# Attention and two expert layers in one kernel: first weight splits of a block placed earlier, and the repeat rounds put under a condition

## The chip, the cores and the metric

The kernel runs on one core of a Trainium2 chip. The metric is device time in microseconds of one execution, the median of three runs; lower is better.

## The reference

Three layers follow each other on 1792 tokens (4 batches of 448) with 768 features; everything is float32, except that the two weights of the first expert layer arrive as float64.

- Attention with 12 heads of 64: `scores = scale * q k^T`, mixed over heads by `w_pre`, softmax, mixed over heads by `w_post`, times `v`.
- First layer ("moe1" in the code): `h = x @ w_in` (768 x 2048), `g = h - tanh(h)`, `x = g @ w_out` (2048 x 768).
- Second layer ("moe2"): every token goes to one of 8 experts (the largest of 8 logits); `out = gate * (relu(x @ w1[e]) @ w2[e])` with 1024 hidden features.

## The kernel before, in words

Most operands are split in a high and a low part (`x = hi + lo`), and one product becomes three matmuls: hi times hi, hi times lo, lo times hi. ScalarE (ACT) writes the high part by a copy, VectorE (DVE) or GpSimd (POOL) subtracts it from the original.

**Attention** ends with a stretch called `window(3)`: 6 pairs of heads, 24 matmuls each (L304). ACT evicts each result twice (L309, L311), POOL subtracts (L312), SyncE (SP) stores both parts to `xd` in DRAM (L357).

**moe1** works in four blocks of tokens (512, 512, 512, 256), and each block in 16 units `f`, one for each 128 hidden features. For unit `f`: `first(b, f)` (L623) is 18 matmuls of `x` with `w_in` (L628) into one of two PSUM banks; `shape(b, f, h)` (L631) computes `h - tanh(h)` by four ACT operations (L638 to L641) and six DVE operations (L642 to L650), and splits the result (ACT L654, POOL L655 in block 0); `second(b, f)` (L665) is 18 matmuls with `w_out` (L672). The loop at L909 runs over the units; in the pass of unit `i` it issues `first` and `shape` of unit `i` and `second` of unit `i - 2`. The bank of `h` is given back when DVE has done L643 of that unit, and `first` two units later writes it again.

Block 0 also brings the weights in. `load_wi(f)` (L475) starts two loads, `wih` and `wil`, the parts of `w_in` that attention stored. `load_wo(f)` (L489) starts the load of `w_out` as float64 into `wor`, of which there is one buffer (only units 1, 14 and 15 have other room), and converts it to float32 by three DVE operations (`convert_f64`, L74: L77, L79, L81); the next `wor` load starts when L81 has read the buffer. `split_wo(0, f)` (L506) then makes `whl`: ACT L509 copies, DVE L510 subtracts.

**What sets the order.** Each engine works its instructions in one fixed order. A scheduler in the language picks it: an instruction takes the place of its line in the program, `tc.high_priority(offset=n)` moves it forward by n instructions, `tc.issue_after(x)` puts it behind `x` where both are on one engine, and otherwise it goes where the scheduler's own estimate has it ready. Before the loop, L570 to L578 issue with priority 300: `x` of block 0, `w_in` of units 0 and 1, `w_out` of units 0 and 1 with their conversions. `split_wo(0, 0)` (L907) and `split_wo(0, 1)` (L920, in the pass of unit 0) come with no priority. `prepare_turn` (L614, in the pass of unit 1) has six small PE transposes (L617) of the expert embedding and one DVE copy of them (L621) with priority 150. `behind(n)` (L500) puts what it holds behind the n-th last unit that was shaped.

**moe2** gathers the tokens of each expert and works through `one_round` (L1003). Each engine's last instructions are those of L1264 and L1267: `count(25, 1)` loads a flag from SBUF into a register of each engine, and a loop that runs zero or one times holds nine inner loops with further rounds, for experts with more tokens than the windows hold. With these inputs the flag is zero, and the loop is passed over. The last work before it is the scatter of output rows by POOL (L1159).

Of the kernel before, what the change touches and what calls it, by code (L numbers as in the profile page):

```python
# [11 lines left out]
F32 = mybir.dt.float32  # L12
# [3 lines left out]
I64 = mybir.dt.int64  # L16
AF = mybir.ActivationFunctionType
ALU = mybir.AluOpType
# [6 lines left out]
DM = H * D  # L25
# [3 lines left out]
FC = DFF // 128  # L29
# [420 lines left out]
def moe1(tc, ctx, bank, xd, wind, sums, w_out, emb, tau, consts, yg, pos, keep, ids0, chosen, w12):  # L450

    nc = tc.nc
    lasting, weights = ExitStack(), ExitStack()

    def pool(name, bufs, side):
        stack = lasting if side == "left" else weights
        return stack.enter_context(tc.tile_pool(name=name, bufs=bufs, side=side, reuse_waits="tile"))
# [3 lines left out]
    pv, pw = pool("m1v", 1, "right"), pool("m1w", 1, "right")  # L461
# [3 lines left out]
    X, G, Y, YT, W = {}, {}, {}, {}, {}  # L465
    wih, wil, wo = {}, {}, {}
# [22 lines left out]
    def load_wo(f):  # L489
        raw = W.get(("raw", f))  # L490
        if raw is None:
            raw = pv.tile([128, DM], I64, tag="wor", name=f"wor_{f}")
            chosen["wor"] = nc.sync.dma_start(out=raw, in_=w_out[f])
        wo[f] = (pw if f < FC - 1 else p1).tile([128, DM], F32, tag=f"wo{f}", name=f"wo_{f}")
        with behind(9 if f > FC - 3 else 99):
            chosen["wo", f] = convert_f64(nc, raw, wo[f])

    steps = []

    def behind(n):  # L500
        order = ExitStack()
        for x in steps[-n] if len(steps) >= n else ():
            order.enter_context(tc.issue_after(x.ins))
        return order

    def split_wo(b, f):  # L506
        if b == 0:
            w = p3.tile([128, 2, DM], F32R, tag="whl", name=f"whl_{b}_{f}")
            nc.scalar.copy(w[:, 0], wo[f])  # L509
            nc.vector.tensor_tensor(out=w[:, 1], in0=wo[f], in1=w[:, 0].bitcast(F32), op=ALU.subtract)  # L510
            W[b, f] = w[:, 0], w[:, 1]
        elif b == 1:
            if f in (0, FC - 4, FC - 2):
                W["pairs"] = p3.tile([128, 2, DM], F32R, tag="whl", name=f"whl_{b}_{f}")
            if 0 < f < FC - 4:
                w = pw.tile([128, DM], F32, tag=f"wo{f - 1}", name=f"wp_{f}")
            else:
                w = W["pairs"][:, f % 2]
            w = w.bitcast(F16)
            W[b, f] = w[:, :DM], w[:, DM:].bitcast(BF)  # L520
            with behind(2):
                nc.scalar.copy(W[b, f][0], wo[f])
                nc.gpsimd.tensor_tensor(out=W[b, f][1], in0=wo[f], in1=W[b, f][0], op=ALU.subtract)
        else:
            W[b, f] = W[1, f]
# [5 lines left out]
    def weigh(f):  # L531
        nc.scalar.activation(out=sq.bitcast(BF), in_=wih[f].rearrange("p a b -> p (a b)"), func=AF.Square,
                             accum_out=room[:, f:f + 1])
# [36 lines left out]
    with tc.high_priority(offset=300):  # L570
        load_x(0)
        load_wi(0)
        load_wi(1)
        load_wo(0)
        raw = px.tile([128, CC, 512], BF, tag="xl", name="wor_1")
        W["raw", 1] = raw.rearrange("p a b -> p (a b)").bitcast(I64)[:, :DM]
        nc.sync.dma_start(out=W["raw", 1], in_=w_out[1])
        load_wo(1)  # L578

    sq = cp.tile([128, DM], F16, tag="sq", name="sq")  # L580
    rt = cp.tile([128, 2], F32, tag="rt", name="rt")
    en = cp.tile([128, CC, 32], F32, tag="en", name="en")
# [31 lines left out]
    def prepare_turn():  # L614
        pt = bank(0, CC - 1, 6)
        for c in range(CC):
            nc.tensor.transpose(pt[:, 8 * c:8 * c + 8], em[:, 128 * c:128 * c + 128], ident[:8, :8])  # L617
        with tc.high_priority(offset=150):
            with tc.issue_after(chosen["wo", 1].ins):
                nc.vector.memset(en, 0.0)  # L620
            nc.vector.tensor_copy(en[:, :, :8], pt[:, :48].rearrange("p (a b) -> p a b", b=8))  # L621

    def first(b, f):  # L623
        N = BLOCKS[b][1]
# [279 lines left out]

    chosen["kept"] = {}
    units = [(b, f) for b in range(len(BLOCKS)) for f in range(FC)]
    split_wo(0, 0)  # L907
    todo = []
    for i, (b, f) in enumerate(units):  # L909
        if b == 0 and 0 < f < FC - 1:  # L910
            load_wo(f + 1)
        with tc.issue_after(chosen["wor"].ins):
            if b == 0 and f + 2 < FC:
                load_wi(f + 2)
            if f == 2 and b + 1 < len(BLOCKS):
                load_x(b + 1)
            if b == 0 and f == 3:
                load_last()
        if i + 1 < len(units):
            split_wo(*units[i + 1])  # L920
        h = first(b, f)
        with tc.issue_after(chosen["wo", 1].ins):
            if b == 0 or f != 1:
                shape(b, f, h)
        if b == 0 and 3 <= f < FC - 1:
            for k in (2 * f - 6, 2 * f - 5) if f < 7 else (f + 1,):
                with behind(2):
                    weigh(k)
        if b + 1 < len(BLOCKS) and 8 <= f < 8 + CC:
            with behind(2):  # L930
                highest(b + 1, f - 8)
        if b + 1 < len(BLOCKS) and f == FC - 2:
            with behind(2):
                bound(b + 1)
        if i == 1:
            prepare_turn()
            for t, src in ((rt[:, 0:1], tau), (lt, tri_d)):
                nc.sync.dma_start(out=t, in_=src)
        if i == 4:
            with behind(2):  # L940
                prepare()
        if todo and (b != 1 or f > 5):
            g, a = todo.pop(0)
            g(*a)
        if i >= 2:
            second(*units[i - 2])
            if units[i - 2][1] == FC - 1:
                with ExitStack() as order:
                    for x in drain(units[i - 2][0]):
                        order.enter_context(tc.issue_after(x.ins))  # L950
                    shape(b, f, h)
                todo = routing(units[i - 2][0])
        for _ in range(1 if b < len(BLOCKS) - 1 else 2):
            if todo and f >= (6 if b == 1 else 2):
                g, a = todo.pop(0)
                g(*a)
        if b == len(BLOCKS) - 1 and f == 5:
            fetch_early()
        if b == len(BLOCKS) - 1 and 6 <= f < 10:
            with behind(2):  # L960
                split_early(2 * (f - 6))
                split_early(2 * (f - 6) + 1)
        if i == len(units) - 3:
            assert not todo
            weights.close()
        if i >= len(units) - 3:
            yield
# [11 lines left out]
def moe2(tc, ctx, bank, ident, yg, pos, keep, ids0, chosen, w12, out, before):  # L979
    nc = tc.nc  # L980
# [22 lines left out]
    def one_round(lists, wins, offs, nm, before=None):  # L1003
# [70 lines left out]
        def split(e, f, j):  # L1074
            if wins[e] == LATE or (before and (e, f, j) in early):
                RW[e, f, j] = kept[f, j]
                return
            raw = RW[e, f, j]
            if before and e == 0:
                wh, wl = lasting(f, j)  # L1080
            else:
                wh = p3.tile([128, DM], F16, tag=f"wh{j}", name=f"wh{j}_{nm}_{e}_{f}")
                wl = p3.tile([128, DM], BF, tag=f"wl{j}", name=f"wl{j}_{nm}_{e}_{f}")
            nc.scalar.copy(wh, raw)  # L1084
            pool_part = (f, j) in ((2, 1), (3, 0), (4, 0), (6, 1)) if before and e == 0 else (f + 2 * j) % 4 == 0
            s = (nc.gpsimd if pool_part else nc.vector).tensor_tensor(out=wl, in0=raw, in1=wh, op=ALU.subtract)  # L1086
            if pool_part:
                chosen["pool"] = s
            RW[e, f, j] = (wh, wl)

        def first(e, f):
# [45 lines left out]
        OR, sent = {}, []  # L1137
# [27 lines left out]
        units = [(e, f) for e in range(E) for f in range(MF)]  # L1165
# [10 lines left out]
        def behind(*ins):  # L1176
            order = ExitStack()
            for x in ins:
                if x is not None:
                    order.enter_context(tc.issue_after(x.ins))  # L1180
            return order
# [17 lines left out]
        for i, (e, f) in enumerate(units):  # L1199
# [1 line left out]
            if f == 0 and e + 1 < E and e + 1 < len(lists):  # L1201
                gather(e + 1)
            if before and e == E - 1 and f == 0:
                with behind(chosen["pool"], sent[-1]):
                    nc.gpsimd.drain(fusable=False)
            if i + 1 < len(units):
                with ExitStack() as order:
# [55 lines left out]
    def count(i, top):  # L1263
        return nc.values_load(keep[0:1, i:i + 1], min_val=0, max_val=top,  # L1264
                              skip_runtime_bounds_check_because="a count of comparisons")

    with tc.For_i(0, count(25, 1)):  # L1267
        for i, (k, n) in enumerate(wins):
            with tc.For_i(0, count(16 + ranks[i], NMORE)) as rd:
                one_round([lists[i]], [MORE], [k * n + rd * MW], f"b{i}")  # L1270
# [94 lines left out]
```

## Time and profile before

| | us |
|---|---|
| median of three runs | 1212.46 (1210.51 to 1213.22) |
| the profiled execution | 1210.71 |
| its span, first to last instruction | 1208.9 |
| TensorE busy in the span | 1162.2 (96%) |
| VectorE busy | 851.1 (70%) |
| ScalarE busy | 748.2 (62%) |
| GpSimd busy | 560.9 (46%) |

The mean granted clock of TensorE over the span is 0.992 of full speed. How to read it: the span is 1.8 us shorter than the time of its own execution, and that execution was 1.75 us faster than the median. Attention takes the first 458 us or so, moe1 lies between 441 and 928 us with its block 0 up to about 602 us, moe2 takes the rest. Busy shares are means over all stages; what a stage waits for is read from the timeline of that stage.

### The profile page before, as it was taken

The numbers are of one execution on the slowest core, as the hardware profiler recorded it, in microseconds if no ns is written. First come the engines' busy times: TensorE is split into PE (matmuls) and PEld (weight loads), VectorE is DVE, ScalarE is ACT, GpSimd is POOL, SyncE is SP. The second block draws the span as 40 slices with busy tenths as digits, with TensorE's granted clock in tenths as the row PEclk, the third lists the DMA queues.
The fourth block names the chain that finished last, engine by engine and source line by source line (L and its number), as shares of the span: only waits on it lengthen the run. The fifth ranks groups of instructions, "written<-read, shape, count | busy, mean of one in ns | idle before, by whom it ended". The sixth has DMA issues, their size and how long they took to land. (4 is left out here: it accounts for less than half of the span.)

```text
span 1208.9 us, 23922 instructions
## 1 busy us (share of the span) xinstructions
PE 1162.2 (96%) x8648; PEld 773.1 (64%) x8648; DVE 851.1 (70%) x2002; ACT 748.2 (62%) x1554; POOL 560.9 (46%) x514
## 2 busy tenths in 40 slices
PE   8999999999999988999999999999999899999996
PEld 3655655665565664665644444544787778899994
DVE  5888779778877875999766766565676655566772
ACT  6887688778868754655565655554577334555661
POOL 3897588678858772111334322111223233344431
PEclk8999999999999999999999999999999999999998
DMA  6465667566665465533100020010034656678760
GB/s 204 148 208 174 195 196 212 163 192 195 195 191 172 151 199 169 206 120 129 55 1 1 1 81 1 1 53 3 2 121 171 215 194 198 212 251 270 248 239 24
DMA packets 84601, 174.13 MB, mean 144 GB/s; under 512 B 12747, under 2 KB 62155, under 8 KB 84472
## 3 DMA queue, kind: packets, MB, share of 16 engines
q1 hardware_dynamic: 78730, 160.95, 40.8%
q0 software_dynamic: 5472, 11.43, 3.5%
q8 instruction: 70, 1.15, 0.4%
q14 instruction: 59, 0.48, 0.2%
q10 hardware_dynamic: 270, 0.12, 0.0%
HBM read 110.98 MB, written 23.30 MB: 111 GB/s over the span
## 5 line engine op out<-in xcount | busy, mean ns | idle before, releaser
L294 POOL TENSOR_TENSOR at<-at 128x480 f16<-128x480 f32 x180 | 179.6, 1008 | 41.3 <-ACT at L293 37.7
L239 PE MATMUL bank<-G,wmix 120*120 120x448 f32 x360 | 171.1, 560 | 8.6 <-DMA G<-S 8.6
L289 PE MATMUL bank<-wr,A 120*128 120x120 f32 (+4 forms) x1800 | 169.9, 242 | 5.4 <-DVE wr L271 4.1
L660 POOL TENSOR_TENSOR ghl<-g,ghl 128x512 bf16<-128x512 f32 (+1 forms) x48 | 48.3, 1006 | 221.5 <-ACT ghl L659 191.1
L249 ACT ACTIVATE A<-bank,st 120x448 f32<-120x448 f32 x180 | 114.9, 638 | 51.7 <-DVE st L243 24.8
L243 DVE TENSOR_REDUCE st<-bank 120x1 f32<-120x448 f32 x180 | 111.6, 620 | 49.5 <-PE bank L239 47.4
L672 PE MATMUL bank<-ghl,whl 128*128 128x512 f32 (+2 forms) x558 | 124.1, 374 | 2.6 <-POOL ghl L655 1.4
L628 PEld LDWEIGHTS <-wih 128*128 128x128 f16 x768 | 73.8, 98 | 74.1 <-issue 10.1
L293 ACT COPY at<-bank 128x480 f32<-128x480 f32 x180 | 101.7, 567 | 29.4 <-PE bank L289 29.1
L1084 ACT CAST wh_a<-wr_a 128x768 f16<-128x768 f32 x112 | 92.6, 829 | 40.2 <-PE bank L1122 33.5
L672 PE MATMUL bank<-ghl,wp 128*128 128x512 f16 (+3 forms) x594 | 113.3, 344 | 1.4 <-POOL ghl L660 1.1
L289 PEld LDWEIGHTS bank<-wr,A 120*128 120x128 f32 (+1 forms) x720 | 90.6, 191 | 37.1 <-issue 19.1
L1086 DVE TENSOR_TENSOR wl_a<-wr_a,wh_a 128x768 bf16<-128x768 f32 x84 | 83.3, 992 | 30.4 <-ACT wh_a L1084 30.1
L254 POOL TENSOR_TENSOR A<-A 120x448 f16<-120x448 f32 (+1 forms) x90 | 85.2, 946 | 28.5 <-ACT A L249 15.0
L642 DVE SCALAR_TENSOR_TENSOR g<-bank,u 128x512 f32<-128x512 f32 (+1 forms) x64 | 39.8, 622 | 81.1 <-ACT d L639 76.9
L658 ACT ACTIVATE g<-g,scales 128x512 f32<-128x512 f32 (+1 forms) x48 | 31.2, 650 | 96.5 <-DVE g L650 83.3
L672 PEld LDWEIGHTS <-wp 128*128 128x128 f16 (+1 forms) x594 | 57.9, 98 | 49.0 <-issue 2.2
L628 PE MATMUL bank<-mxh,wih 128*128 128x512 f16 (+1 forms) x384 | 84.5, 357 | 4.3 <-DVE d L643 4.3
L1122 PE MATMUL bank<-rh_a,wl_a 128*128 128x208 f16 (+5 forms) x336 | 86.2, 260 | 0.0
L1122 PE MATMUL bank<-rl_a,wh_a 128*128 128x208 bf16 (+5 forms) x336 | 86.2, 260 | 0.0
L1098 PE MATMUL bank<-xph_a,wh_a 128*128 128x208 f16 (+5 forms) x336 | 86.2, 259 | 0.0
L1122 PE MATMUL bank<-rh_a,wh_a 128*128 128x208 f16 (+5 forms) x336 | 86.2, 259 | 0.0
(249 smaller groups left out, 2758.8 us busy)
## 6 DMA issues: line engine op xcount, KB each, us to landing
wr_a<-in_w_dram SPq DMA_DIRECT2D x62, 768.0 KB
G<-S SPq DMA_DIRECT2D x176, 210.0 KB
raw_w<-in_w_in_dram SPq DMA_DIRECT2D x32, 384.0 KB
wor<-in_w_out_dram SPq DMA_DIRECT2D x14, 768.0 KB
raw_v<-in_v_dram SPq DMA_DIRECT2D x16, 384.0 KB
yg<-row SPq DMA_DIRECT2D x3, 1540.0 KB
raw_q<-in_q_dram SPq DMA_DIRECT2D x9, 448.0 KB
raw_k<-in_k_dram SPq DMA_DIRECT2D x9, 448.0 KB
```

The source lines that it names most:

```text
L239: nc.tensor.matmul(ps[:r, :S], wmix[:r, :r], g[:r], start=True, stop=True)
L243: latest["dve"] = nc.vector.tensor_reduce(out=st[:r, k:k + 1], in_=ps[:r, :S], axis=AX.X, op=ALU.min)
L249: latest["act"] = nc.scalar.activation(out=a[:r, :S], in_=ps[:r, :S], func=AF.Exp, bias=bias, scale=-1.0, accum_out=st[:r, 4 + k:5 + k])
L254: nc.gpsimd.tensor_tensor(out=parts[1][:r, :S], in0=a[:r, :S], in1=parts[0][:r, :S], op=ALU.subtract)
L289: nc.tensor.matmul(ps[:, jc * r:jc * r + r], x[:r, js], w[:r].rearrange("p (a b) -> p a b", b=10)[:, :, :n], start=(i == 0), stop=(i == le ...
L293: nc.scalar.copy(at32[:, :, t0:t0 + n], v)
L294: nc.gpsimd.tensor_tensor(out=atl[:, :, t0:t0 + n], in0=at32[:, :, t0:t0 + n], in1=ath[:, :, t0:t0 + n], op=ALU.subtract)
L628: nc.tensor.matmul(h, u[f][:, c], X[b][v][:, c, :N], start=(i == 0), stop=(i == len(seq) - 1))
L672: chosen["second"] = nc.tensor.matmul(Y[b][c][:, :N], w[u][:, 128 * c:128 * c + 128], hl[v], start=(f == 0 and i == 0), stop=(f == FC - 1 ...
L1084: nc.scalar.copy(wh, raw)
L1098: nc.tensor.matmul(h, w[u][:, 128 * c:128 * c + 128], XP[e][v][:, c, :N], start=(i == 0), stop=(i == len(seq) - 1))
L1122: nc.tensor.matmul(O[e][c][:, :N], w[u][:, 128 * c:128 * c + 128], r[v], start=(f == 0 and i == 0), stop=(f == MF - 1 and i == 2))
```

## The change

The splits of units 0 and 1 move into the high-priority stretch before the loop, together with the loads of `w_in` and `w_out` for unit 2; the loop no longer issues these. The conversion of `w_out` for unit 2 is put behind the shaping of unit 0. All of `shape` is put behind both splits (on ACT and DVE), and the DVE copy of the transposed embedding behind the last DVE operation of unit 0. The loop around the further rounds becomes a condition, with the rounds as the block that is placed next. The key `"pool"` is renamed `"low"` where it held an instruction, which changes nothing that runs.

```diff
@@ load_wo
-        with behind(9 if f > FC - 3 else 99):
+        with behind(9 if f > FC - 3 else 1 if f == 2 else 99):
             chosen["wo", f] = convert_f64(nc, raw, wo[f])
@@ split_wo
             w = p3.tile([128, 2, DM], F32R, tag="whl", name=f"whl_{b}_{f}")
-            nc.scalar.copy(w[:, 0], wo[f])
-            nc.vector.tensor_tensor(out=w[:, 1], in0=wo[f], in1=w[:, 0].bitcast(F32), op=ALU.subtract)
+            chosen["split", f] = (nc.scalar.copy(w[:, 0], wo[f]), nc.vector.tensor_tensor(
+                out=w[:, 1], in0=wo[f], in1=w[:, 0].bitcast(F32), op=ALU.subtract))
@@ in the stretch with priority 300
         load_wo(1)
+        load_wi(2)
+        W["raw", 2] = pv.tile([128, DM], I64, tag="wor", name="wor_2")
+        chosen["wor"] = nc.sync.dma_start(out=W["raw", 2], in_=w_out[2])
+        split_wo(0, 0)
+        split_wo(0, 1)
@@ prepare_turn
-            nc.vector.tensor_copy(en[:, :, :8], pt[:, :48].rearrange("p (a b) -> p a b", b=8))
+            with tc.issue_after(steps[0][0].ins):
+                nc.vector.tensor_copy(en[:, :, :8], pt[:, :48].rearrange("p (a b) -> p a b", b=8))
@@ the loop over units
-    split_wo(0, 0)
...
-            if b == 0 and f + 2 < FC:
+            if b == 0 and 0 < f < FC - 2:
                 load_wi(f + 2)
...
-        if i + 1 < len(units):
+        if 0 < i < len(units) - 1:
             split_wo(*units[i + 1])
         h = first(b, f)
-        with tc.issue_after(chosen["wo", 1].ins):
-            if b == 0 or f != 1:
+        if b == 0 or f != 1:
+            with ExitStack() as order:
+                for x in chosen["split", 0] + chosen["split", 1]:
+                    order.enter_context(tc.issue_after(x.ins))
                 shape(b, f, h)
@@ moe2, the end
-    with tc.For_i(0, count(25, 1)):
+    more = count(25, 1)
+    with tc.If(more > 0, preferred_fallthrough_block=True):
         for i, (k, n) in enumerate(wins):
```

## Rows read from the trace of the kernel before

**Rows 1.** The page, part 1: busy time, share of the span, instructions
```profile
PE 1162.2 (96%) x8648; PEld 773.1 (64%) x8648; DVE 851.1 (70%) x2002; ACT 748.2 (62%) x1554; POOL 560.9 (46%) x514
```

**Rows 2.** Stretches of 5 us: busy of PE, PEld, DVE, ACT, POOL; clock, DMA, GB/s
```profile
455.00:460.00 5.00, 5.00 (x44) 2.88 (x39) 0.22 (x1) 1.96 (x4) 2.45 (x5) 1.00 0.28 93
...
465.00:470.00 5.00, 1.11 (x9) 0.72 (x9) 3.33 (x6) 2.54 (x4) 0.00 (x0) 0.92 0.22 81
470.00:475.00 5.00, 3.91 (x11) 1.29 (x10) 5.00 (x9) 2.90 (x4) 1.28 (x1) 0.73 0.09 16
```

**Rows 3.** Timeline of PE, block 0: start, length, what, [idle before, releaser]
```profile
464.93 0.54 PE L617 MATMUL bank<-ident,em_stage 8*128 8x8 f32 x6
469.36 2.72 PE L628 MATMUL bank<-mxh,wih 128*128 128x512 f16 x6 [3.89 <-DVE d L643]
...
488.69 1.47 PE L628 MATMUL bank<-mxh,wih 128*128 128x512 f16 x6
...
496.70 1.47 PE L628 MATMUL bank<-mxh,wih 128*128 128x512 f16 x6
```

**Rows 4.** Timeline of DVE, from the first conversions to unit 0's last step
```profile
449.39 3.52 DVE L81 SCALAR_TENSOR_TENSOR wo<-wor,wo 128x768 uint32<-128x768 uint32 x2
458.60 0.22 DVE L620 MEMSET en<- 128x192 f32 x1 [5.70 <-POOL bp L569]
462.27 0.69 DVE L642 SCALAR_TENSOR_TENSOR g<-bank,u 128x512 f32<-128x512 f32 x1 [3.45 <-ACT d L639]
465.50 0.21 DVE L621 COPY en<-bank 128x48 f32<-128x48 f32 x1 [2.54 <-PE bank L617]
466.88 1.83 DVE L510 TENSOR_TENSOR whl<-wo,whl 128x768 fp32r<-128x768 f32 x2 [1.16 <-ACT whl L509]
468.62 0.68 DVE L643 SCALAR_TENSOR_TENSOR d<-bank,d 128x512 f32<-128x512 f32 x1
...
472.10 0.73 DVE L650 COPY_PREDICATED g<-u,d 128x512 f32<-128x512 int32 x1
```

**Rows 5.** Timeline of PE's weight loads, the first of unit 2
```profile
466.53 0.10 PEld L628 LDWEIGHTS <-wih 128*128 128x128 f16 x1 [1.16 <-DMA wih<-wind]
```

**Rows 6.** Timeline of SP: loads of float64 weights for units 3, 9 and 13
```profile
473.69 0.33 SPq L493 DMA_DIRECT2D wor<-in_w_out_dram  x1
...
526.43 0.33 SPq L493 DMA_DIRECT2D wor<-in_w_out_dram  x1
...
559.39 0.33 SPq L493 DMA_DIRECT2D wor<-in_w_out_dram  x1
```

**Rows 7.** Timeline of DVE, the conversion of unit 9
```profile
530.91 0.82 DVE L77 TENSOR_SCALAR wo<-wor 128x768 uint32<-128x768 uint32 x1 [1.09 <-DMA wor<-in_w_out_dram]
```

**Rows 8.** Waits of DVE, 475 to 600 us: total, times, longest
```profile
DVE wo L77 <- DMA wor<-in_w_out_dram: 2.3, 4, 1.1
```

**Rows 9.** Timeline of PE, block 0, `second` of unit 10
```profile
557.61 4.15 PE L672 MATMUL bank<-ghl,whl 128*128 128x512 f32 x17 [0.52 <-POOL ghl L655]
```

**Rows 10.** Timeline of POOL, the last scatter
```profile
1198.50 0.93 POOL L1159 DMA_INDIRECT out_dram<-or_a,oi_a  x1 [5.92 <-ACTq L1267]
```

**Rows 11.** Line 1267 in stretches of 1 us: ns min/median/max, first and last start
```profile
L1267 PEldq COMPARE_BRANCH  x1: 3867/3867/3867, 1197.4 to 1197.4; - x1
...
L1267 POOLq COMPARE_BRANCH  x1: 53/53/53, 1198.9 to 1198.9; - x1
...
L1267 POOLq EVENT_SEMAPHORE  x3: 43/43/43, 1201.7 to 1201.9; - x3
...
L1267 POOLq COMPARE_BRANCH  x1: 41/41/41, 1202.3 to 1202.3; - x1
...
L1267 POOLq EVENT_SEMAPHORE  x9: 43/43/43, 1205.3 to 1206.0; - x9
...
L1267 POOLq COMPARE_BRANCH  x1: 33/33/33, 1207.6 to 1207.6; - x1
```

**Rows 12.** DMA queues, 1202 to 1203 us: packets, MB, share of 16 engines
```profile
q14 instruction: 2, 0.02, 6.7%
```

More of the change, by code (lines that the diff above doesn't have):

```diff
@@ L1087, in split @@
             if pool_part:
-                chosen["pool"] = s
+                chosen["low"] = s
             RW[e, f, j] = (wh, wl)
@@ L1203, in one_round @@
             if before and e == E - 1 and f == 0:
-                with behind(chosen["pool"], sent[-1]):
+                with behind(chosen["low"], sent[-1]):
                     nc.gpsimd.drain(fusable=False)
```

## The prediction

> **What bounds the kernel now.** The page comes first: TensorE is busy 96% of the span [rows 1], so time can only come from the few places where it stands still. The waits of PE by stretch lead to the one large place after attention, the start of moe1, and the table of 5 us stretches shows it: from 465 to 470 us PE is busy 1.11 us, from 470 to 475 us 3.91 us, at a mean granted clock of 0.92 and 0.73 between its levels of 1.2 and 2.4 GHz, where it was 1.00 before the stop [rows 2]. The second place is the end: POOL finishes its scatter at 1199.43 us [rows 10], yet the span goes on to 1208.9.
>
> The timeline of PE tells what the first place costs. The six small transposes end at 465.47; the first matmul of unit 2 starts at 469.36, held 3.89 us by DVE's L643, which gives the PSUM bank of unit 0 back. At 488.69 `first` of unit 4 starts. In between lie two `first` and two `second`, 72 matmuls. One of each, from 488.69 to 496.70, takes 8.01 us, so 16.0 of these 23.2 us are work, and **7.2 us** are lost to the stop, to the lower clock and to late operands [rows 3].
>
> The timeline of DVE tells why. ACT's `d` let L642 run at 462.27, so L643 could have followed at about 462.9. But the embedding's copy stood ahead of it and waited 2.54 us for PE's transposes, then both splits, which waited 1.16 us for ACT's copies and took 1.7; L643 came at 468.62. Meanwhile DVE had stood idle 5.70 us before 458.60 and 3.45 us before 462.27, with both conversions done by 452.91 [rows 4]. The `w_in` of unit 2 was late too: PE's weight load waited for it until 466.53 [rows 5].
>
> A third reading decides how much of the 7.2 us stays. In the middle of block 0 the loads of float64 weights follow each other in a loop, conversion, load, conversion. From unit 9 to 13 four turns take 32.96 us, 8.24 each [rows 6], longer than PE's 8.01. The load takes 4.48 us (526.43 to 530.91), the conversion among `shape`'s steps the rest, and DVE sometimes waits for the load [rows 7, 8]. By unit 10 PE has no lead left: `second` waits 0.52 us for `ghl` [rows 9]. So at the end of this stretch PE can be only as much earlier as this loop is.
>
> **The change, part by part.**
>
> *Splits, copy, order.* The two splits move into DVE's and ACT's idle time. From 455 to 460 us ACT is busy 1.96 of 5 us and DVE 0.22 [rows 2], and they need 1.83 us of DVE [rows 4] and about as much of ACT. POOL's memset at about 458.5, for which DVE's L620 waited, suggests that the room of moe1's left pools comes free only when attention's last matmuls end. Then the splits run from 458.5 to 462, still ahead of L642. If they start earlier, ACT's copies stand between evictions of attention with over half of ACT free; I price that at nothing, at most at 1 us. L643 then comes at 462.9, 5.7 us earlier, and `first` of unit 2 starts behind the transposes at about 465.5. Unit 0's last step, L650, comes 3.5 us after L643, as before (472.10 less 468.62), so it ends at 463 + 3.5 + 0.7 = 467 or sooner. The embedding's copy follows it; its bank is used only by the sixth group of `second`, over 4 us later, so it costs nothing.
>
> *Loads of unit 2.* Two loads of `w_in`, 192 KB each, and one of float64 weights move ahead on SP. The first two end the wait of 1.16 us [rows 5], which lay inside the 3.89 us. The third waits for the conversion of unit 0, at worst until 452.91 [rows 4], with attention's stores behind it on SP; their data is read in later blocks, so I take nothing, and 1 us as the bound.
>
> *Conversion of unit 2.* It waits for L650 of unit 0 and needs 2.4 us of DVE, with up to 1.2 us of unit 1's steps between: it ends at 469 to 470.5. The load of unit 3 followed it at 473.69 [rows 6], and so moves forward by 3.2 to 4.7 us; a shorter unit 0 would add about 1. I take **4.7 us** for this loop and, by the third reading, for block 0. The bounds are 0, if the loop keeps its place, and 7.2, if it closes up. Behind block 0 PE is busy nearly throughout and its inputs shift with it, so the gain stays.
>
> *The condition at the end.* POOL's sequence before: a branch at 1198.9, then waits for the scatter's landing until 1201.9, a branch at 1202.3, nothing until 1205.3, semaphore instructions to 1206.2, nothing until a branch at 1207.6, the end at 1208.9 [rows 11]. The first pause, 3.0 us, is a far jump over the rounds: two packets of instructions were fetched on a queue at that moment [rows 12], and PE's branch of the same kind took 3.87 us, hidden at 1197.4 behind the wait for the scatter [rows 11]. With the rounds placed next, the far jump must be the first branch, at 1198.9, ahead of the wait; 3.0 us later it is 1201.9, just when the scatter has landed. I take 3.0 for that pause and 1.0 of the 1.4 and 0.9 us behind it, **4.0 us**. The bounds are 0 and 5.3: after 1202.3 nothing is left then but the 1.3 us from 1207.6 to the end.
>
> The trace gives the branches themselves 33 to 53 ns on POOL [rows 11] and the pause behind the second 3.0 us. The Trainium skill, Advanced Engine Details and Errata, section Control Flow Timing, has a compare-and-branch at about 108 ns; by that figure alone moving the branch gives 0.1 us at the end, and the sum would be 4.8 instead of 8.7, an estimate from that page.
>
> **Sum:** 4.7 + 4.0 = 8.7 us. Against the profiled execution, 1210.71, that is 1202.0; it ran 1.75 us under the median shown. On the median of 1212.46 it is **1203.8 us**.
>
> **The rivals.** A measurement of this kernel tells 0.2% from no change, 2.4 us: faster is under 1210.0, slower over 1214.9.
>
> *The loop keeps its place.* PE gains 7 us at unit 2 and gives them back as waits for `ghl` in units 5 to 12, because the conversions stay where they were. For it: the 8.24 against 8.01 us and the wait of 0.52. Against it: the loop's start hangs on unit 0's steps, which move. Block 0 then gives 0.8, the sum is 4.8, the time 1207.7.
>
> *The jump is not hidden.* POOL makes a far jump behind the scatter's landing after all, or one more on the way to the end. Against it: POOL's first branch stands ahead of the landing. The time is 1212.46 - 4.7 = 1207.8. The rule of the Trainium skill, Runtime: NRT & Kernel Launch, section Instruction fetch mechanics, speaks for it: a taken branch to code that is not held stalls until it is fetched, and with the rounds next it is the path always taken here that jumps. The 3.0 and 3.87 us agree with the rule; whether the wait hides them no row shows.
>
> *Nothing moves.* The scheduler keeps the splits behind unit 0's steps or trades one stop for another, and the end keeps its pauses: 1211.5.
>
> *Slower: DVE stands before its loads.* DVE's order in block 0 is written anew. If each conversion now stands before more of `shape` and reaches its load sooner, DVE idles there, and it has no time to spare. Before, it waited 2.3 us in all [rows 8]. There are 11 conversions from unit 3 on; an added wait of 0.8 us each uses up the 8.7 us, and at 1.2 us each the time is 1212.46 + 13.2 - 8.7 = 1217. Against it: the same rules order these steps as before, and the load and what stands behind it shift together.
>
> **How the numbers follow.** Forecast 0.58, loop 0.14, jump 0.14, nothing 0.08, slower 0.06. The time is the forecast's. Its own bounds reach from 1212.46 - 7.2 - 5.3 = 1200.0 to about 1206.5; the two half gains at 1207.7 and 1207.8, with their spread, take the range to 1209. What is left out above is 0.14 and a little of the half gains, below almost nothing. Faster: 0.58 and most of 0.28, 0.85. Same: 0.08. Slower: 0.07.
>
> **What would show it.** Right: DVE's L643 at about 463 and no wait of several us ahead of PE's unit 2; a granted clock of 1.00 from 465 to 475; the load of unit 3 at 469 to 470.5; at the end POOL's 3 us pause between its first branch and the landing, and about 4 us from landing to end instead of 7. Wrong: waits of PE for `ghl` that grow from unit 5 on, longer waits of L77 for `wor`, attention ending later than 458.4, or a pause of 3 us behind the landing.

## The result, and the profile after

The kernel after takes **1201.61 us** (median of six runs, 1198.34 to 1203.3) against 1212.38 for the kernel before beside it: a ratio of 0.9909, 95% interval [0.9892, 0.9927], a gain of 8.8 to 13.1 us. The forecast was 1203.8, with a range of 1200.0 to 1209.0. Further runs of the same kernel (e14, below) gave 0.9908 [0.9887, 0.993].

Lines of after: the transposes are L622, `first` L634, `shape` L644 to L656 (L643 of before is L649, L650 is L656), its high part L660 and low part L661, `second` L678, the embedding's copy L627, both halves of a split L509, the scatter L1166, the condition L1275.

The profiled execution of after took 1202.62 us, span 1200.8, against 1210.71 and 1208.9. The difference of 8.1 us has four parts, between marks that both traces have:

| stretch | before | after | difference |
|---|---|---|---|
| start to the transposes of block 0 | 464.93 | 465.96 | +1.03 |
| transposes to `second` of block 1 ("block-0 stretch") | 141.11 | 135.77 | -5.34 |
| from there to the last scatter's start | 592.46 | 593.17 | +0.71 |
| the scatter's start to the end of the span | 10.4 | 5.9 | -4.5 |

Nothing in the runs ties the first and the third part to the change; the second and the fourth are told below.

**Block 0.** The timeline of PE of the kernel after, as [rows 3]: start, length, what, and in brackets the idle time before and its releaser:

```profile
465.96 0.53 PE L622 MATMUL bank<-ident,em_stage 8*128 8x8 f32 x6
467.99 4.24 PE L634 MATMUL bank<-mxh,wih 128*128 128x512 f16 x11 [1.49 <-DMA wih<-wind]
...
485.69 1.47 PE L634 MATMUL bank<-mxh,wih 128*128 128x512 f16 x6
```

The stop of 3.89 us is now 1.49, and it is for `w_in`, no longer for DVE. From the end of the transposes (466.49) to `first` of unit 4 are 19.2 us with 16.0 of work: 3.2 us lost instead of 7.2. About half of that is the clock, as in [rows 2]:

```profile
465.00:470.00 5.00, 3.51 (x16) 1.44 (x15) 3.36 (x7) 2.67 (x5) 0.00 (x0) 0.81 0.42 163
470.00:475.00 5.00, 5.00 (x21) 2.35 (x20) 4.96 (x7) 1.32 (x3) 1.28 (x1) 0.85 0.00 0
```

The timeline of DVE, as [rows 4], shows the planned order: both splits, then unit 0's steps, with the bank's release (L649) at 463.91; unit 0's last step (L656), the copy, and the conversion of unit 2 follow. The L648 at 467.18 is unit 1's; it stands ahead of unit 0's last two steps and waits 1.64 us for ACT:

```profile
461.26 2.10 DVE L509 TENSOR_TENSOR whl<-wo,whl 128x768 fp32r<-128x768 f32 x2 [1.42 <-ACT whl L509]
463.30 0.69 DVE L648 SCALAR_TENSOR_TENSOR g<-bank,u 128x512 f32<-128x512 f32 x1
463.91 0.68 DVE L649 SCALAR_TENSOR_TENSOR d<-bank,d 128x512 f32<-128x512 f32 x1
...
467.18 0.69 DVE L648 SCALAR_TENSOR_TENSOR g<-bank,u 128x512 f32<-128x512 f32 x1 [1.64 <-ACT d L645]
...
468.99 0.72 DVE L656 COPY_PREDICATED g<-u,d 128x512 f32<-128x512 int32 x1
469.60 0.20 DVE L627 COPY en<-bank 128x48 f32<-128x48 f32 x1
469.71 0.55 DVE L77 TENSOR_SCALAR wo<-wor 128x768 uint32<-128x768 uint32 x1
```

The timeline of SP, the loads for units 2, 3 and 13 (compare [rows 6]):

```profile
462.13 0.38 SPq L581 DMA_DIRECT2D wor<-in_w_out_dram  x1
462.56 0.45 SPq L480 DMA_DIRECT2D wih<-wind  x1
...
474.03 0.33 SPq L493 DMA_DIRECT2D wor<-in_w_out_dram  x1
...
556.89 0.33 SPq L493 DMA_DIRECT2D wor<-in_w_out_dram  x1
```

The load of unit 3 has hardly moved forward: 8.07 us behind the transposes, 8.76 before. Yet unit 13's comes 90.93 behind them instead of 94.46. The loop gained 2.8 us on its way; DVE's waits for the loads fell from 2.3 us [rows 8] to 0.4, and PE has no wait at all from 475 to 600 us, where before had 0.52 at unit 10 [rows 9] and 0.25 at unit 12.

**The end.** The last scatter, then line 1275 in stretches of 1 to 2 us (ns min/median/max, first and last start), as [rows 10, 11]:

```profile
1194.90 0.93 POOL L1166 DMA_INDIRECT out_dram<-or_a,oi_a  x1 [5.91 <-ACT or_a L1161]
```
```profile
L1275 PEldq COMPARE_BRANCH  x1: 3789/3789/3789, 1193.0 to 1193.0; - x1
...
L1275 POOLq COMPARE_BRANCH  x1: 58/58/58, 1195.2 to 1195.2; - x1
...
L1275 POOLq EVENT_SEMAPHORE  x1: 17/17/17, 1198.0 to 1198.0; - x1
...
L1275 POOLq INC_SWDGE_SEM  x1: 240/240/240, 1198.5 to 1198.5; - x1
```

POOL branches once, 0.3 us after the scatter's start; its next instruction comes 2.8 us later, about when the scatter lands (3.2 us after its start before). No pause follows, and the span ends 2.8 us after 1198.0.

### The profile page after: what moved, and what is told of

The parts are those of the page before. It is cut to its first block, busy times and chain, and to the rows that moved or that the text cites. A ratio compares the mean times of both kernels' runs of the same rounds, so it can differ in the third digit from the quotient of the medians.

```text
span 1200.8 us, 23863 instructions
## 1 busy us (share of the span) xinstructions
PE 1167.1 (97%) x8648; PEld 776.2 (65%) x8648; DVE 844.7 (70%) x2002; ACT 746.7 (62%) x1554; POOL 562.8 (47%) x514
## 3 DMA queue, kind: packets, MB, share of 16 engines
q8 instruction: 70, 1.15, 0.5%
## 5 line engine op out<-in xcount | busy, mean ns | idle before, releaser
L678 PE MATMUL bank<-ghl,whl 128*128 128x512 f32 (+2 forms) x558 | 123.0, 373 | 0.8 <-POOL ghl L666 0.5
L293 ACT COPY at<-bank 128x480 f32<-128x480 f32 x180 | 101.6, 566 | 30.7 <-PE bank L289 30.3
L634 PEld LDWEIGHTS <-wih 128*128 128x128 f16 x768 | 73.9, 98 | 71.9 <-issue 7.4
L289 PEld LDWEIGHTS bank<-wr,A 120*128 120x128 f32 (+1 forms) x720 | 91.7, 193 | 36.7 <-issue 19.2
L678 PE MATMUL bank<-ghl,wp 128*128 128x512 f16 (+3 forms) x594 | 113.3, 344 | 1.4 <-POOL ghl L666 1.1
L648 DVE SCALAR_TENSOR_TENSOR g<-bank,u 128x512 f32<-128x512 f32 (+1 forms) x64 | 39.9, 623 | 76.0 <-ACT d L645 72.4
L678 PEld LDWEIGHTS <-wp 128*128 128x128 f16 (+1 forms) x594 | 57.9, 98 | 49.0 <-issue 2.2
L634 PE MATMUL bank<-mxh,wih 128*128 128x512 f16 (+1 forms) x384 | 84.9, 358 | 1.9 <-DMA wih<-wind 1.5
```

What stands on the lines that cost most here:

```text
L289: nc.tensor.matmul(ps[:, jc * r:jc * r + r], x[:r, js], w[:r].rearrange("p (a b) -> p a b", b=10)[:, :, :n], start=(i == 0), stop=(i == le ...
L293: nc.scalar.copy(at32[:, :, t0:t0 + n], v)
L634: nc.tensor.matmul(h, u[f][:, c], X[b][v][:, c, :N], start=(i == 0), stop=(i == len(seq) - 1))
L678: chosen["second"] = nc.tensor.matmul(Y[b][c][:, :N], w[u][:, 128 * c:128 * c + 128], hl[v], start=(f == 0 and i == 0), stop=(f == FC - 1 ...
```

## The experiments

Marks as in the table above; the stretches come from one profiled execution each. They are what the experiments rest on, since the times don't tell the variants of the kernel after apart. e3, e4, e5 and e10 ran once each and took 1203.44, 1200.67, 1200.47 and 1202.46 us, beside 1210.04 for before: e4 and e5, whose block-0 stretches are longer than after's, come out under its median of 1201.61. The part from block 1 to the last scatter, which no edit touches, alone ran from 589.6 us (e4) to 593.9 (e14).

**e1: the end alone.** Before, with only this edit. Against before on one chip:

```diff
-    with tc.For_i(0, count(25, 1)):
+    more = count(25, 1)
+    with tc.If(more > 0, preferred_fallthrough_block=True):
```


> The kernel before with the condition at the end alone. If the far jump is now taken ahead of the scatter's landing, the stretch from the start of the last scatter to the end of the span falls from 10.4 us to about 5.9 as in the changed kernel, and the time by 4.5 us (my sum had 4.0), a ratio near 0.9963; block 0 keeps its stop of 3.9 us. If the end's gain in the changed kernel came from elsewhere (a different state of the queues after a shorter block 0), the stretch stays above 9 us and the ratio is 0.999 to 1.001.

Measured: 1208.35 us, ratio 0.9973 [0.996, 0.9987], a gain of 1.6 to 4.9 us; scatter to end 5.78 us, block-0 stretch 140.25 with the stop of 3.89 us still there. The end is worth 4.6 us by itself.

**e2: block 0 alone.** After, with the loop at the end put back (the diff of e1 reversed).

> All of the change but the condition: the loop around the further rounds is back. My sum had 4.7 us for block 0, the changed kernel's trace shows 5.3 from the end of the transposes to block 1; so 4.7 to 6.3 us under the kernel before, a ratio of 0.9948 to 0.9961, and 10.4 us again from the last scatter's start to the end. If the two parts are not independent, the two single gains do not add up to the 10.8 us of the whole change.

Measured: 1204.66 us, ratio 0.995 [0.9933, 0.9967]; a gain of 4.0 to 8.1 us; block-0 stretch 135.84, scatter to end 10.4. The gains of the two medians, 3.5 us (e1) and 7.2, add up to 10.7 beside the 10.8 of the whole change, so nothing shows that the halves touch each other.

**e7, e15: unit 3's `w_in` early as well.** After, with its loads ahead of the float64 weights of unit 2; e15 is the same kernel again, beside e14.

```diff
         load_wi(2)
+        load_wi(3)
         W["raw", 2] = pv.tile([128, DM], I64, tag="wor", name="wor_2")
...
-            if b == 0 and 0 < f < FC - 2:
+            if b == 0 and 1 < f < FC - 2:
```


> The changed kernel with the two loads of w_in for unit 3 also ahead of the float64 load for unit 2. Theory order: PE's fixed order has unit 3's first matmuls ahead of unit 2's, so the wait of 1.49 us for w_in was unit 3's; it goes, but the next matmuls, unit 2's, need the bank of unit 1, free about 469.0 in the changed kernel's clock, so PE waits there for L649 instead, 0.5 to 1.2 us, and the gain is 0.3 to 1.5 us on the changed kernel. Theory loop (my third reading): nothing at the start counts, since the conversions decide; gain 0. Theory load alone: the whole 1.5 us and the low clock after it go, 3 us.

> The kernel of e7_wi3_early (after, with unit 3's w_in loaded ahead of unit 2's float64 weights) again, beside after on one chip. Stretch from the transposes to block 1: 133.9 in its one profile, 135.8 in after. Theory ORDER OF LOADS (the wait of 1.5 us for w_in and the lower clock behind it are what after still loses at the start): 133.6 to 134.2 again, and the time 0.997 to 0.9995 of after's. Theory CHANCE (the 1.9 us came from that one execution): 135 to 136.

Measured: block-0 stretch 133.89 and 133.92; 1199.8 us, ratio 0.9915 [0.9894, 0.9936], and 1200.68, 0.9896 [0.987, 0.9921]. The timeline of PE in e7 (lines shifted by one):

```profile
466.56 1.47 PE L635 MATMUL bank<-mxh,wih 128*128 128x512 f16 x6
469.26 1.46 PE L635 MATMUL bank<-mxh,wih 128*128 128x512 f16 x6 [1.23 <-DVE d L650]
```

The wait for `w_in` is gone, although unit 2's was early already. So it was unit 3's `w_in` that PE waited for: in PE's order unit 3's first matmuls stand ahead of unit 2's, as they did before. SP's timeline of before agrees, with `w_in` of unit 2 and of unit 3:

```profile
448.60 0.42 SPq L480 DMA_DIRECT2D wih<-wind  x1
...
461.53 0.45 SPq L480 DMA_DIRECT2D wih<-wind  x1
```

[rows 5] waited until 466.53, 5.0 us after the second of these and 17.9 after the first. What is left in e7 is 1.23 us for the bank of unit 1, which unit 2 writes: about the stop that theory order had (0.5 to 1.2).

**e14: after once more**, beside e15 and e13.

> After itself, once more, on the same chip as the next two, so that they can be set against it. Expected: 0.989 to 0.993 of before; stretch from the transposes to block 1 135.5 to 136.1 us, from the last scatter's start to the end 5.7 to 6.1.

Measured: 1201.47 us, ratio 0.9908 [0.9887, 0.993], scatter to end 5.86, but a block-0 stretch of **134.13**, below what I expected. PE's wait is about the same, 1.42 us. The row of the matmul names another releaser, but the row of its weight load, below it, names `w_in` again:

```profile
466.68 2.67 PE L634 MATMUL bank<-mxh,wih 128*128 128x512 f16 x11 [1.42 <-DVE g L648]
```
```profile
466.68 0.98 PEld L634 LDWEIGHTS <-wih 128*128 128x128 f16 x6 [1.50 <-DMA wih<-wind]
```

The clock stayed up. Stretches of 5 us in e14, as in [rows 2]:

```profile
465.00:470.00 5.00, 3.58 (x20) 1.65 (x19) 4.04 (x8) 2.88 (x5) 0.77 (x1) 1.00 0.17 61
470.00:475.00 5.00, 4.95 (x24) 3.51 (x23) 4.97 (x6) 2.11 (x4) 0.58 (x2) 1.00 0.20 55
```

The eleven matmuls behind the wait took 2.67 us, not 4.24. So the same stop sometimes costs 1.6 us of clock on top: in after, e2 and e10 (135.77, 135.84, 135.82) and not in e14. Of e15's expected theories, ORDER OF LOADS holds for the wait, and the stretch lies in its range; but the gain is small: 133.92 against 134.13 with the clock up is 0.2 us, most of the 1.9 us between e7 and after was after's clock, and the medians (1200.68, 1201.47) can't be told apart.

**e8: banks in the units' order**, so that unit 2 takes unit 0's bank and PE takes it first; **e13: with unit 3's `w_in` early too.**

```diff
-        h = bank(6)[:, :N]
+        h = (bank(6) if b else bank(6, f + 1))[:, :N]
```


> The changed kernel with the banks of block 0's first products taken by unit number, so that unit 2 writes the bank of unit 0 and unit 3 that of unit 1. Theory order: PE's order then has unit 2 first, whose weights and bank are ready, and no stop is left after the transposes; what the changed kernel still loses there, 3.2 us (1.49 us of waiting and the low granted clock behind it), goes: 3 us under the changed kernel, about 0.9885 of the kernel before. Theory loop: units 5 to 12 have no more than 1.6 us of lead of the shaped data over PE's need, so PE waits for it (waits on POOL's subtraction) and the gain is at most 1.6 us. Rival to both: the scheduler's new order stops elsewhere, no gain.

> After with both: unit 3's w_in early, and the banks of h in the order of the units, so that unit 2 takes unit 0's bank. Theory START (what PE loses at the start is all that is left to gain): no wait behind the transposes, granted clock 1.00, stretch 132.5 to 133.3. Theory SLACK (the shaped data have 1.6 us of lead in after and no more): PE starts at once, but waits for ghl in units 2 to 6, 1 us or more in all, and the stretch is 133.5 to 135.8, no better than with the early load alone.

Measured: e8 1200.35 us, ratio 0.9915 [0.9895, 0.9935], stretch 135.69; e13 1201.54, 0.9914 [0.9892, 0.9936], stretch 135.06. In both PE starts right behind the transposes at a clock of 1.00, and then waits elsewhere; e13:

```profile
471.82 4.19 PE L679 MATMUL bank<-ghl,whl 128*128 128x512 f32 x17 [0.86 <-POOL ghl L662]
...
512.59 2.60 PE L679 MATMUL bank<-ghl,whl 128*128 128x512 f32 x10 [0.40 <-POOL ghl L662]
```

The two rows are waits for the low parts of units 0 and 5; a third, 0.33 us for a bank, comes at 581.18. SLACK holds in the main. In after POOL ends unit 5's low part at 511.84, 1.6 us ahead of PE's `second` of unit 5 (513.44). e7, e14 and e15 use about this lead up without a wait; in e13 the low part comes 0.65 us later against the transposes than in after, and PE waits. The longer wait, unit 0's, SLACK didn't have: PE comes to `second` of unit 0 before its low part is done. e8 has the same waits (0.87, 0.85 and 0.49 us), and its stretch is no shorter than after's: of its theories the rival holds, that the new order stops elsewhere.

**e5: the embedding's copy without its order.** It stands ahead of unit 0's steps on DVE again.

```diff
-            with tc.issue_after(steps[0][0].ins):
+            with ExitStack():
                 nc.vector.tensor_copy(en[:, :, :8], pt[:, :48].rearrange("p (a b) -> p a b", b=8))
```


> After, but the DVE copy of the transposed embedding without its order, so that it stands ahead of unit 0's last steps as in the kernel before. Stretch from the transposes to the first matmul of block 1 whose operand is ghl: 135.8 us in after, 141.1 in before. DVE should stand some 3 us for PE's transposes (to about 466.2), unit 0's bank come free at about 467.6 and the conversion of unit 2 start some 3 us later. Theory START (block 0's gain is PE's earlier start and nothing else): the bank comes about when unit 3's w_in lands anyway (468.0), so PE's start and the stretch change by 0.5 us at most: 135.3 to 136.3. Theory LOOP (the loop of conversions and loads sets the pace): everything is 3 us later and the stretch is 138.5 to 139. Theory SLACK (the loop has the 1.6 us of lead that the shaped data of unit 5 showed in after): 136.5 to 137.7, with waits of PE for ghl from unit 5 on.

Measured: stretch 137.19, 3.1 us over e14 at the same clock of 1.00. DVE stood 3.17 us for the transposes; PE stopped twice for L649 (1.49 and 1.49 us) and once for `ghl` (1.21). No wait for `ghl` came later, and the load of unit 3 was 8.49 us behind the transposes, not 3 us later than in after. The number fits SLACK, but its mechanism (waits from unit 5 on) isn't what happened: the copy's cost is paid at once. The copy's place is worth 3.1 us of this stretch.

**e4: the conversion of unit 2 without its place.**

```diff
-        with behind(9 if f > FC - 3 else 1 if f == 2 else 99):
+        with behind(9 if f > FC - 3 else 99):
```


> After, but the conversion of w_out for unit 2 without its place behind unit 0's shaping. Theory ORDER (the place matters, as the prediction had it for the loop): the conversion takes DVE as soon as the data has landed (about 466.6) or waits for it, unit 0's last steps come up to 4 us later, and the stretch is 136.8 to 139. Theory FREE (the scheduler puts it behind unit 0's steps anyway): 135.3 to 136.3 and the DVE order of unit 0's steps as in after.

Measured: stretch 137.56 at a clock of 1.00, 3.4 us over e14: ORDER holds. But not for the reason I had for it. The load of unit 3 came 3.1 us *earlier* (SP's timeline of e4; unit 13's below):

```profile
470.96 0.33 SPq L493 DMA_DIRECT2D wor<-in_w_out_dram  x1
...
556.83 0.33 SPq L493 DMA_DIRECT2D wor<-in_w_out_dram  x1
```

and unit 13's stood at 90.88 us behind the transposes, as in after (90.93). The head start was used up, and PE waited, behind 1.33 us for `w_in`, for `ghl` at the start (0.97 and 0.72 us) and again at units 10 and 12:

```profile
555.04 4.15 PE L678 MATMUL bank<-ghl,whl 128*128 128x512 f32 x17 [0.53 <-POOL ghl L661]
...
571.60 3.69 PE L678 MATMUL bank<-ghl,whl 128*128 128x512 f32 x15 [0.27 <-POOL ghl L661]
```

**e3: the early `w_in` of unit 2 undone.**

```diff
-        load_wi(2)
...
-            if b == 0 and 0 < f < FC - 2:
+            if b == 0 and f < FC - 2:
```


> After, but the two loads of w_in for unit 2 back in the loop, as in the kernel before. My prediction gave the early loads the end of a wait of 1.16 us. Theory NONE (that wait was for unit 3's w_in, since PE takes unit 3 first, so the early load of unit 2's ended nothing): the stretch from the transposes to block 1 stays at 135.3 to 136.3, and PE's wait behind the transposes is still for w_in or for unit 0's bank, 1 to 2 us. Theory LOAD (the early load is worth that wait): 136.9 or more, with a wait of PE for w_in of 2.5 us or more.

Measured: stretch 137.49, with a wait of 2.17 us for `w_in` and the clock at 0.66 from 470 to 475 us. That is 1.7 us over the executions of after with a lowered clock: nearer to LOAD, and NONE falls. SP now issued the two loads of `wih` at 463.52 and 465.57, by the loop's order unit 2's and then unit 3's, while before had unit 2's at 448.60. PE went on at 469.61, when the second had landed; the weight load at which it stood names that load's semaphore in the trace. So it is unit 3's `w_in` again that PE waits for, and unit 2's ahead of it makes it some 2 us later against the transposes than in after. DVE's conversions take longer as well (28.1 us for ten, 24.6 in after; see below), so the 1.7 us isn't the load's alone.

**e10: the rounds not preferred as next.**

```diff
-    with tc.If(more > 0, preferred_fallthrough_block=True):
+    with tc.If(more > 0, preferred_fallthrough_block=False):
```


> After, but with the rounds not preferred as the block placed next. From the start of the last scatter to the end of the span: 10.4 us in before, 5.9 in after. Theory PLACE (with the rounds next, the one far jump falls ahead of the scatter's landing; with the rounds far, it falls elsewhere): if the way past the rounds still needs a jump, POOL's pause of about 3 us comes behind the landing and the stretch is 8 to 10 us; if it needs none, no pause is seen on POOL and PE's branch of 3.8 us is gone too, with the stretch at 5 to 6 us. Theory IF (that a condition stands in place of a loop does it, whatever is placed next): 5.7 to 6.1 us with the same pauses of PE (3.8) and POOL (2.8) ahead of the landing.

Measured: scatter to end 7.61 us, a little under what PLACE had. POOL branches at 1193.1 and goes on at once; a second branch follows the scatter's landing (line 1275, then the next POOL instruction, of line 1369):

```profile
L1275 POOLq EVENT_SEMAPHORE  x3: 17/17/17, 1193.2 to 1193.4; - x3
...
L1275 POOLq COMPARE_BRANCH  x1: 48/48/48, 1193.1 to 1193.1; - x1
...
L1275 POOLq EVENT_SEMAPHORE  x3: 43/43/43, 1196.1 to 1196.2; - x3
...
L1275 POOLq COMPARE_BRANCH  x1: 41/41/41, 1196.6 to 1196.6; - x1
```
```profile
L1369 POOLq DRAIN  x2: 106/240/373, 1199.2 to 1199.8; - x2
```

From 1196.6 to 1199.2 POOL stands 2.6 us with nothing left to hide it. So there is one far jump either way, and the placement decides on which side of the landing it falls. Of the 4.5 us, 2.8 come from a condition in place of the loop (10.4 to 7.6) and 1.7 from the placement (7.6 to 5.9).

## Why the prediction was right, and where its steps were not

**Right in the numbers.** Block 0 gave 5.3 us for a predicted 4.7 (7.0 against e14, whose clock stayed up), the end 4.5 for 4.0, the time fell inside the range, and each half alone (e1, e2) gives its part. For the end this is the mechanism; for block 0 it is partly luck, since the step from which the 4.7 was taken did not happen (below).

*Splits, copy, order: right.* DVE split behind attention's last matmuls, L649 came at 463.91, 2.05 us ahead of the transposes' start (before, L643 came 3.69 behind it). e5 shows that the copy's place carries 3.1 us of the stretch. What the splits' place carries by itself no run shows.

*Loads of unit 2: failed.* "The first two end the wait of 1.16 us": that wait was unit 3's and is still there (1.49). Likewise the bank that PE waited for in [rows 3] was unit 0's, but the unit that wanted it was 3, not 2. I read the unit from the loop and not from PE's own order. The restart came at 467.99, some 1.5 us later against the transposes than I had it, and the clock was 0.81 and 0.85 from 465 to 475 us where I had 1.00; in e14 it was 1.00. The early loads are worth something for another reason: they take unit 2's transfer out of the way of unit 3's (e3).

*Conversion of unit 2, and the third reading: failed.* The step in which the load of unit 3 moves forward by 3.2 to 4.7 us, and with it all of block 0's 4.7, did not happen: the load moved by 0.7 us. Unit 0's last step was to end at 467 or sooner (468 with the 1.03 us by which attention ended later) and ended at 469.71, because unit 1's L648 stood ahead of it and waited 1.64 us for ACT; and the conversion, put at 2.4 us and up to 1.2 of unit 1's steps, took 4.3 (469.71 to 474.01), its L79 alone 2.02 us beside POOL's subtraction. "PE can be only as much earlier as this loop is" fails too: at unit 13 the loop is 3.5 us earlier than before, PE at the end of the stretch 5.3 (7.0 in e14). In e4 the loop stands as in after at unit 13, and PE is 1.8 to 3.4 us later. In its place the stretch can be told from PE's own waits and clock: e7, e14 and e15, all at a clock of 1.00, less their one wait (1.23, 1.42, 1.23) leave 132.66, 132.71 and 132.69 us. The other variants of after lie at that plus their waits and the lower clock to within about 1 us: e5 at 137.19 less 4.19 is 133.0, e4 at 137.56 less 3.82 is 133.7, after at 135.77 less 1.49 less 1.57 of clock (4.24 against 2.67) is 132.7. The 5.3 us are the 4.0 less that PE loses at the start (7.2 to 3.2) and 1.3 at the two stops for `ghl` that went: before took 8.80 us from `second` of unit 10 to that of unit 11 and 8.51 from 12 to 13, in place of 8.01.

Why those went, though the loop started almost where it did, the groups of DVE's lines from 475 to 560 us show (busy us, mean ns, idle before): first before, then after, then e4.

```profile
L79 DVE SCALAR_TENSOR_TENSOR wo<-wor,wo 128x768 uint32<-128x768 uint32 x10 | 10.9, 1087 | 0.1
L81 DVE SCALAR_TENSOR_TENSOR wo<-wor,wo 128x768 uint32<-128x768 uint32 x10 | 10.5, 1047 | 0.1
...
L77 DVE TENSOR_SCALAR wo<-wor 128x768 uint32<-128x768 uint32 x10 | 9.3, 934 | 2.3 <-DMA wor<-in_w_out_dram 2.3
```
```profile
L81 DVE SCALAR_TENSOR_TENSOR wo<-wor,wo 128x768 uint32<-128x768 uint32 x10 | 9.5, 954 | 0.0
L79 DVE SCALAR_TENSOR_TENSOR wo<-wor,wo 128x768 uint32<-128x768 uint32 x10 | 9.5, 953 | 0.0
...
L77 DVE TENSOR_SCALAR wo<-wor 128x768 uint32<-128x768 uint32 x10 | 5.6, 556 | 0.4 <-DMA wor<-in_w_out_dram 0.4
```
```profile
L79 DVE SCALAR_TENSOR_TENSOR wo<-wor,wo 128x768 uint32<-128x768 uint32 x10 | 10.9, 1095 | 0.1
L81 DVE SCALAR_TENSOR_TENSOR wo<-wor,wo 128x768 uint32<-128x768 uint32 x10 | 10.5, 1047 | 0.1
L77 DVE TENSOR_SCALAR wo<-wor 128x768 uint32<-128x768 uint32 x10 | 10.0, 1002 | 1.7 <-DMA wor<-in_w_out_dram 1.7
```

The same ten conversions take 30.7 us of DVE before, 24.6 in after, 31.4 in e4. The placing of one conversion (e4's only edit) put all that follow at another point of the units' steps, where they no longer start beside POOL's subtraction; the last section tells what that costs. PE's waits for `ghl` at units 10 and 12 come only in kernels with long conversions (before, e4, and e3 with 28.1), but long conversions don't always bring them: e1, which has before's block 0, shows none at these units, and PE loses only 0.5 us there (8.27 and 8.23 us in place of 8.01 from unit 9 to 11). That the long steps cause the waits is argued from the traces; no run changed them alone.

*The end: right in the main, mis-sized by 0.5.* The far jump falls ahead of the landing, as the step said, and landing to end is 2.8 us where I had 4 (by my own sum it should have been 3.2, the 7.2 before less 4.0). The term that was too small is the 1.0 us for the 1.4 and 0.9 us behind the first pause: with 3.0 for that pause, 1.5 of them went. The attribution was off: I gave the placement 3.0 us, and it carries 1.7, the condition itself 2.8. The rival in which the jump is not hidden falls: the stalls, 2.8 us on POOL and 3.8 on PE, lie beside the wait for the scatter. The Trainium skill, Runtime: NRT & Kernel Launch, section Instruction fetch mechanics, has a taken branch to code that is not held stall until it is fetched; both stalls agree with it.

*The rivals.* The loop did keep its place at its start, but the waits for `ghl` that this was to bring didn't come. The rival in which DVE idles at its loads fell: 0.4 us.

## What to carry to other kernels

Where one engine is busy 96% of the time, cost a change by the waits of that engine alone, and take which instruction waits from its own order of instructions, not from the order of the source. A new place for one instruction on a shared vector engine can shift everything behind it against the other engines; look for operations whose length differs from their own mean before pricing a loop by its turn. A jump that cannot be avoided belongs ahead of a wait that ends later anyway.

## What was not expected of the hardware

**DVE and POOL hold each other up.** Timelines of DVE and POOL, a conversion of before and one of after:

```profile
547.49 1.65 DVE L77 TENSOR_SCALAR wo<-wor 128x768 uint32<-128x768 uint32 x1 [0.25 <-DMA wor<-in_w_out_dram]
```
```profile
547.45 1.27 POOL L655 TENSOR_TENSOR ghl<-g,ghl 128x512 fp32r<-128x512 f32 x1 [7.45 <-ACT ghl L654]
```
```profile
497.78 0.57 DVE L77 TENSOR_SCALAR wo<-last_wor 128x768 uint32<-128x768 uint32 x1
498.25 0.97 DVE L81 SCALAR_TENSOR_TENSOR wo<-wor,wo 128x768 uint32<-128x768 uint32 x1
499.12 0.97 DVE L79 SCALAR_TENSOR_TENSOR wo<-last_wor,wo 128x768 uint32<-128x768 uint32 x1
500.12 1.93 DVE L81 SCALAR_TENSOR_TENSOR wo<-last_wor,wo 128x768 uint32<-128x768 uint32 x1
```
```profile
497.83 3.41 POOL L661 TENSOR_TENSOR ghl<-g,ghl 128x512 fp32r<-128x512 f32 x1 [6.14 <-PE bank L634]
```

In before, L77 starts 0.04 us after POOL's subtraction and takes 1.65 us instead of 0.55: it ends 0.42 after POOL. All eight conversion steps of over 1 us in before, from 475 to 560 us, start while a subtraction runs. In after the subtraction is the one held: 3.41 us instead of 1.28, ending 1.15 us after the conversion step that ended at 500.09, and the L81 that starts at 500.12 then ends 0.81 after POOL. POOL has time for it, with 1.6 us left at unit 5 (see e13): its low parts took 14.6 us for ten before, 19.4 for eleven in after. The Trainium skill, SBUF — State Buffer, section Who interferes with whom, has VectorE and GpSimd share a pair of ports as an exclusive lock, the second to issue blocking until the first is done. The row of before agrees; in after POOL stayed blocked through three DVE steps that follow each other without a gap (from 497.78).

**The clock differs between executions.** The same stop of about 1.4 us was followed by a granted clock of 0.81 in one execution of after and of 1.00 in e14. In the first 30 us the clock was 0.89 in before's profile and 0.72 in after's, which no edit touches. The 1.03 us by which the transposes came later in after can't be put down to that: profiles with 0.83 in the first 30 us have them from 464.73 us (e14, the kernel after itself) to 466.91 (e3), and e1, with before's attention and block 0, at 466.37. Why the start differs stays open.
